# Linear attention and two feed-forward networks on one core: k-v products and the turning of k with both heads of a pair in one matmul

## Chip, core and metric

The kernel runs on one core of a Trainium2 chip. The metric is the device time of one execution in microseconds. Three runs of the kernel before gave 814.27 to 815.28 us, with a median of 814.49.

## What is computed

The reference, cut to what matters (q, k, v are float32, shaped 4 x 8 x 576 x 64):

```python
q_s = np.exp(q - np.max(q, axis=-1, keepdims=True))
q_s = q_s / (np.sum(q_s, axis=-1, keepdims=True) + 1e-09)
k_s = np.exp(k - np.max(k, axis=2, keepdims=True))
k_s = k_s / (np.sum(k_s, axis=2, keepdims=True) + 1e-09)
kv = np.einsum('bhsd,bhse->bhde', k_s, v)
x = np.einsum('bhsd,bhde->bhse', q_s, kv)       # then 2304 x 512
h = x @ w_in                                    # 512 x 2048
x2 = (h * (1.0 / (1.0 + np.exp(-1.702 * h)))) @ w_out
h = x2 @ w_in2
sp = np.where(h > 20.0, h, np.log1p(np.exp(np.minimum(h, 20.0))))
out = (h * np.tanh(sp)) @ w_out2
```

So k is normalised over the 576 positions of a head, a 64 x 64 product of k and v is made per head, and q times that product is the input of the first network.

## The kernel before

The 2304 rows are cut into five blocks (`SIZES`: 512, 512, 512, 384, 384). Attention makes the input of a block, and the networks then run over blocks of rows and 16 slices of 128 hidden columns. The networks' matmuls are split: each fp32 operand is two fp32r parts, high and low, and three matmuls make one product (`SPLIT`). They are the spine of the program, on TensorE (PE). In the first network a step n computes `gemm_in` (12 matmuls of 512 columns, L1034) and `gemm_out` (12 as well, L1103). Weights arrive as raw words and are decoded by ScalarE (ACT: L451, L415) and VectorE (DVE: L462, L475, L419), and are then split into a high copy (L405, L406) and a low remainder (L398).

Attention's steps are guests on PE between the spine's. Heads are taken in pairs, and a pair of one batch is a unit u; there are 16, of 4 batches with 4 pairs each. k of a unit lies in a tile `kt` with 96 partitions: position p*6 + c goes to partition p, slot c. Its layout is head, slot, element. The steps of a unit are:

- `k_load` (one DMA a unit) and `v_load`, all on SyncE's queue.
- The first three units (`NTURN`) use `k_first`: k is turned by 12 matmuls with the identity (L693), so that the maximum can be taken along a row (L706). ACT applies the exponential with sums (L721), PE turns it back (L732) and ACT copies it to `kt` (L741).
- The other 13 use `k_later`: the maximum is made on DVE over the 6 slots (`k_max`, L666 and L676), PE turns the remaining 96 x 128 maxima (L679), DVE reduces them (L680), PE spreads the result (L753), DVE subtracts it (L755) and ACT applies the exponential (L756).
- `k_kv` multiplies by v on PE (L769): 6 slots times 2 heads, 12 fp32 matmuls. Head j writes partitions 64*j to 64*j + 63. In the units of `k_later`, v has two more columns of ones, which give the sums of k. Then the reciprocal on DVE (L786 to L790) and two scaled copies (L798) into `kv32`, which holds both heads' products on its diagonal.
- `q_turn` turns q (L919, 4 transposes) and `x_part` multiplies it by `kv32` (L949).

Units 0 to 3 belong to the first block and run before the first network's first matmul. The 12 others belong to the blocks 1 to 3 and run as guests.

The order of all steps is not written out. The program first records them (`Plan.op`: possible engines with a cost in ns, what is read, what is written). `Plan.order` then places them engine by engine from the costs, with urgencies that `Plan.best` finds in 20 passes with random noise (`SEED`, `NOISE`). Before the spine starts it fills PE's idle time with idle transposes (L1701). A guest followed by a spine step is charged `RETURN` ns. `FIRST` and `RIGHTS` tell behind which network step the combined weights are made. So a changed cost or constant anywhere moves the order of all engines.

## Time and profile before

| what | value |
|---|---|
| runs shown, median (lowest to highest) | 814.49 us (814.27 to 815.28) |
| profiled execution, its own time | 812.75 us |
| its span, from first to last instruction | 811.0 us |
| PE matmul busy | 803.3 us (99%), 5082 records |
| PE weight loads busy | 731.9 us (90%) |
| VectorE (DVE) busy | 654.0 us (81%) |
| ScalarE (ACT) busy | 455.5 us (56%) |
| GpSimd (POOL) busy | 17.9 us (2%) |
| DMA | 208.57 MB, mean 257 GB/s |
| mean granted clock of PE, as a share | 0.999 |

Times are in microseconds. A busy engine is one on which some instruction is under way. Matmuls overlap, so their mean duration is longer than the time from one start to the next, and the second is what a matmul costs in a stream. An fp32 matmul is two records, an fp32r matmul or a transpose one. The first number of a tile shape such as 96*64 is the contraction's partitions, the second the weight's columns, and the shape behind it is the moving operand. In the timeline a row is a start, a length, and a group of like instructions with their count.

### The profile page before, as it was taken

What the parts mean: (1) busy time and instruction counts of PE and PEld (TensorE: products, weight loads), DVE (VectorE), ACT (ScalarE), POOL (GpSimd) and SP (SyncE); (2) the same over time, 40 slices, a digit from 0 to 9 for tenths busy, and PEclk for the clock granted to TensorE, in tenths of its full rate; (3) what the DMA queues carried; (4) which work ended last, traced back from release to release, by engine and by line L of the source; (5) the groups of instructions that cost most, each with busy time, mean ns of one, the idle gap of its engine ahead of it and who ended that gap; (6) DMA issues with size and microseconds to landing.
All of it is one profiled execution on the core that took longest, in us unless ns stands there. A gap on an engine that the chain in (4) does not pass through costs nothing.

```text
span 811.0 us, 14340 instructions
## 1 busy us (share of the span) xinstructions
PE 803.3 (99%) x5082; PEld 731.9 (90%) x5082; DVE 654.0 (81%) x1269; ACT 455.5 (56%) x887; POOL 17.9 (2%) x23
## 2 busy tenths in 40 slices
PE   8999999999999999999999999999999999999998
PEld 7787778877788888999999999999999999999998
DVE  7999987999966888776779779978677987677964
ACT  6998954556664565745557546555344663344542
POOL 0001000001000000000000000000000021000000
PEclk9999999999999999999999999999999999999999
DMA  9788875847777889988987998999698886778762
GB/s 248 231 258 241 266 255 166 250 136 202 233 254 263 264 264 320 319 283 264 301 264 268 293 321 274 308 318 385 179 286 298 299 293 214 227 251 265 270 195 59
DMA packets 127959, 208.57 MB, mean 257 GB/s; under 512 B 38736, under 2 KB 88464, under 8 KB 127888
## 3 DMA queue, kind: packets, MB, share of 16 engines
q1 hardware_dynamic: 127888, 207.66, 79.3%
q8 instruction: 40, 0.66, 0.3%
q14 instruction: 31, 0.25, 0.1%
HBM read 152.57 MB, written 55.05 MB: 256 GB/s over the span
## 4 chain that ended last, share of the span: by engine, by line
PE 84%; DVE 3%; DMA 1%; issue 0%; ACT 0%; DVEq 0%
PE acc L1557 22%; PE at L1327 18%; PE acc L1103 11%; PE h L1034 11%; PE h L1327 10%; PE acc L1666 5%; PE h L1666 3%; PE at L949 1%; PE at L769 1%; DMA raw<-in_moe_w_out_dram 1%; PE at L919 1%; DMA combos<-raw 1%; PE h L1557 0%; DVE kt L755 0%; DVE g L398 0%
## 5 line engine op out<-in xcount | busy, mean ns | idle before, releaser
L1034 PE MATMUL h<-xt,wi 128*128 128x512 f32 x576 | 145.0, 396 | 0.0
L1103 PE MATMUL acc<-g,wo 128*128 128x512 f32 x576 | 144.3, 394 | 0.0
L1557 PE MATMUL acc<-wi,second 128*128 128x256 f32 x1116 | 137.5, 283 | 0.0
L1557 PEld LDWEIGHTS acc<-wi,second 128*128 128x128 f32 x1116 | 135.6, 192 | 0.0
L1034 PEld LDWEIGHTS h<-xt,wi 128*128 128x128 f32 x576 | 106.5, 188 | 23.1 <-issue 1.0
L1103 PEld LDWEIGHTS acc<-g,wo 128*128 128x128 f32 x576 | 106.8, 188 | 22.7 <-issue 1.0
L1327 PE MATMUL at<-xt,wi 128*128 128x384 f32 x612 | 119.0, 335 | 0.1
L1327 PEld LDWEIGHTS at<-xt,wi 128*128 128x128 f32 x612 | 106.8, 188 | 2.8 <-DVE gt L1379 0.4
L1349 ACT ACTIVATE quad<-quad 128x384 f32<-128x384 f32 x96 | 50.2, 525 | 86.4 <-DVE quad L1379 85.8
L406 ACT ACTIVATE second<-quad 128x384 fp32r<-128x384 f32 x126 | 65.1, 523 | 47.2 <-PE acc L1557 41.8
L398 DVE TENSOR_TENSOR second<-quad,second 128x384 fp32r<-128x384 f32 x125 | 71.6, 577 | 16.3 <-ACT second L406 16.2
L1327 PE MATMUL h<-xt,wi 128*128 128x384 f32 x348 | 65.9, 334 | 0.0
L398 DVE TENSOR_TENSOR quad<-quad 128x384 f32<-128x384 f32 x96 | 53.0, 556 | 13.5 <-ACT quad L1349 11.8
L1327 PEld LDWEIGHTS h<-xt,wi 128*128 128x128 f32 x348 | 60.8, 188 | 0.0
L406 ACT ACTIVATE raw<-dec 128x512 fp32r<-128x512 f32 (+1 forms) x64 | 37.1, 600 | 20.5 <-DVE dec L398 14.8
L1327 PE MATMUL at<-wi,wi 128*128 128x384 f32 x246 | 48.3, 335 | 0.0
L1557 PE MATMUL acc<-wi,g 128*128 128x256 f32 x372 | 48.2, 283 | 0.0
L451 ACT ACTIVATE dec<-raw 128x512 f32<-128x512 f32 x62 | 41.1, 666 | 10.8 <-DMA raw<-in_moe_w_in_dram 5.5
L475 DVE CUSTOM_DVE_ANT_0 dec<-raw,dec 128x1024 uint16<-128x1024 uint16 x64 | 44.9, 703 | 1.7 <-ACT raw L415 0.2
L1557 PEld LDWEIGHTS acc<-wi,g 128*128 128x128 f32 x372 | 46.2, 192 | 0.0
L1327 PEld LDWEIGHTS at<-wi,wi 128*128 128x128 f32 x246 | 43.2, 188 | 1.0 <-DVE gt L1379 0.3
L1057 ACT ACTIVATE gt<-h 128x512 f32<-128x512 f32 x41 | 24.2, 591 | 31.9 <-PE h L1034 31.0
(191 smaller groups left out, 1158.1 us busy)
## 6 DMA issues: line engine op xcount, KB each, us to landing
wi<-combos SPq DMA_DIRECT2D x96, 512.0 KB, 4.9
wi<-outs SPq DMA_DIRECT2D x76, 512.0 KB, 5.6
raw<-in_moe_w_in_dram SPq DMA_DIRECT2D x32, 512.0 KB, 5.3
raw<-in_moe_w_out_dram SPq DMA_DIRECT2D x32, 512.0 KB, 5.4
combos<-raw SPq DMA_DIRECT2D x32, 512.0 KB, 4.1
outs<-raw SPq DMA_DIRECT2D x32, 256.0 KB, 3.8
wi<-combos SPq DMA_DIRECT2D x32, 256.0 KB, 5.2
combos<-raw SPq DMA_DIRECT2D x24, 256.0 KB, 3.8
```

What stands on the lines that cost most here:

```text
L398: return lambda: engine.tensor_tensor(out=out(), in0=in0(), in1=in1(), op=op)
L406: (ACT, act_ns(n), lambda: nc.scalar.activation(out=out(), in_=in_(), func=AF.Copy), False),
L451: lambda: nc.scalar.activation(out=f32(a), in_=f32(hi_w), func=AF.Prelu, scale=2.0**-112, alpha=2.0**32),
L475: dve(512, [rl], [da], lambda: nc.vector.tensor_tensor(out=a, in0=a, in1=lo_w, op=ALU.add), pair=True)
L769: nc.tensor.matmul(out=ps3[j * D : (j + 1) * D, 0:width], lhsT=of[:, j, c, :], rhs=w[:, j, c, :], start=c == 0, stop=c == KC - 1,)
L1034: nc.tensor.matmul(out=h(), lhsT=w_mm(fc, 0, a, cc), rhs=x_of(t)[:, cc, b, :], start=cc == 0 and i == 0, stop=cc == NCC - 1 and i == 2,)
L1057: act(nb, [hk, ("tables",)], [tk], lambda: nc.scalar.activation(out=t, in_=h, func=AF.Tanh, scale=0.851), psum=True)
L1103: nc.tensor.matmul(out=acc[dm][:, 0:nb], lhsT=w_mm(fc, 1, a, dm), rhs=g_of(n)[:, b, :], start=fc == 0 and i == 0, stop=fc == NFC - 1 and i ...
L1327: nc.tensor.matmul(out=bank_of(key)[:, 0:NB], lhsT=wt(fc, 0)[:, w : w + P], rhs=operand(k, b)[:, cc, :], start=cc == 0 and i == 0, stop=cc ...
L1349: nc.scalar.activation(out=t(), in_=t(), func=AF.Mish if n >= NPR else AF.Gelu_apprx_sigmoid)
L1557: nc.tensor.matmul(out=bank_of(banks[c])[:, at_ : at_ + 256], lhsT=slot(pr, a)[:, c * P : c * P + P], rhs=rhs(b), start=pr == 0 and i == 0 ...
L1666: nc.tensor.matmul(out=o, lhsT=w_mm(2 * n + j, 1, a, dm), rhs=g_tile(n, j)[:, b, lo:hi], start=n == 0 and j == 0 and i == 0 and (c < 4 or ...
```

## The change

Both heads of a pair stand side by side in `kt` (slot, head, element), so that one slot of both is a 96 x 128 weight. The turning of k takes that weight in one transpose per slot, 6 in place of 12 matmuls. The k-v product takes it against v of both heads side by side (128 columns, or 130 with the ones between the heads), 6 matmuls in place of 12; the two blocks off the diagonal are not read. k is loaded by one DMA per head. The planner's cost of a turning falls from 180 to 84 ns a slot, `q_turn` and `x_part` are exempt from the charge for a return (`light`), and constants of the planner, `FIRST` and `RIGHTS` differ.

```diff
-    NOISE = 400
+    NOISE = 700
...
-    RETURN = 100
+    RETURN = 90
...
                 if guests and i in self.spine:
-                    cost += self.RETURN
-                guests = guest(i)
+                    cost += 0.0 if last in self.light else self.RETURN
+                guests, last = guest(i), i
...
-    kt = [ap.tile([KP, 2, KC, D], F32, name=f"kt{i}") for i in range(2)]
+    kt = [ap.tile([KP, KC, 2, D], F32, name=f"kt{i}") for i in range(2)]
...
-    vt = ap.tile([KP, 2, KC, D + 2], F32, name="vt")
+    vt = ap.tile([KP, KC, 2 * D + 2], F32, name="vt")
...
+    vs = {u: sp.tile([KP, KC, 2 * D + 2], F32, name=f"vs{u}") for u in range(max(NTURN, 1), NHP - 1)}
...
     def k_load(u, begun):
         b, hp = divmod(u, NHP)
-        dma(
-            S * 512,
-            begun,
-            [("kt", k_tile(u))],
-            lambda: kt[k_tile(u)],
-            lambda: k[b, 2 * hp : 2 * hp + 2].rearrange("h (p c) d -> p h c d", c=KC),
-            slow=1.35,
-        )
+        for j in range(2):
+            dma(
+                S * 256,
+                begun,
+                [k_keys(u)[j]],
+                lambda j=j: kt[k_tile(u)][:, :, j, :],
+                lambda j=j: k[b, 2 * hp + j].rearrange("(p c) d -> p c d", c=KC),
+                slow=1.45,
+            )
...
             def turn(i=i, lo=lo, hi=hi):
                 for c in range(lo, hi):
-                    for j in range(2):
-                        nc.tensor.matmul(
-                            out=ps[i][j * D : (j + 1) * D, (c - lo) * KP : (c - lo + 1) * KP],
-                            lhsT=t[:, j, c, :],
-                            rhs=ident[0:KP, 0:KP],
-                            start=True,
-                            stop=True,
-                        )
-
-            pe(180 * (hi - lo), [kk], [keys[i]], turn, whole=True)
+                    nc.tensor.transpose(
+                        ps[i][:, (c - lo) * KP : (c - lo + 1) * KP],
+                        t[:, c].rearrange("p j d -> p (j d)"),
+                        ident[0:KP, 0:KP],
+                    )
+
+            pe(84 * (hi - lo), k_keys(u), [keys[i]], turn)
...
         def mm():
-            of = t.rearrange("p j c d -> p (j c d)").rearrange("p (c j d) -> p j c d", j=2, c=KC) if first else t
-            w = vd[u] if first else vt
             for c in range(KC):
-                for j in range(2):
-                    nc.tensor.matmul(
-                        out=ps3[j * D : (j + 1) * D, 0:width],
-                        lhsT=of[:, j, c, :],
-                        rhs=w[:, j, c, :],
-                        start=c == 0,
-                        stop=c == KC - 1,
-                    )
+                nc.tensor.matmul(
+                    out=ps3[:, 0:width],
+                    lhsT=t[:, c].rearrange("p j d -> p (j d)"),
+                    rhs=vd[u][:, :, c, :] if first else vs.get(u, vt)[:, c, :],
+                    start=c == 0,
+                    stop=c == KC - 1,
+                )
...
-    RIGHTS = {0: (2,), 1: (3,), 2: (4,), 4: (5,), 5: (6,), 8: (7,)}
+    RIGHTS = {0: (2,), 1: (3,), 2: (4,), 3: (5,), 5: (6,), 8: (7,)}
...
-    FIRST = (13, 16, 17, 18, 21, 22, 23, 24)
+    FIRST = (14, 17, 18, 19, 22, 23, 24, 25)
```

Line numbers of the changed kernel are some units higher: the turning is L703, the k-v product L776, the turning of q L926, the x part L956, `gemm_in` L1041 and `gemm_out` L1110.

How the order moves is shown at three places. The first is PE in the third block's attention, around a k-v product that is a guest of the first network. `acc`, `h` and `at` are PSUM banks, `xt` the block's input, `g` the activated hidden columns, `wi` and `wo` weights, and the last number the count of matmuls. Before:

```order
L1034 MATMUL h_107<-xt,wi_77 128x512 x3
L769 MATMUL at_111<-vt,kt_116 64x66 x12
L919 MATMUL at_112<-ident,qt 128x128 x4
L1034 MATMUL h_107<-xt,wi_77 128x512 x9
L949 MATMUL at_112<-qT_1_125,kv_3_123 128x4x32
```

With the change:

```order
L1041 MATMUL h_106<-xt,wi_78 128x512 x6
L926 MATMUL at_112<-ident,qt 128x128 x4
L776 MATMUL at_111<-vt,kt_116 128x130 x6
L1041 MATMUL h_106<-xt,wi_78 128x512 x6
L1110 MATMUL acc_99<-g,wo_83 128x512 x3
L956 MATMUL at_112<-qT_1_125,kv_3_123 128x4x32
```

Six matmuls of 128 output partitions take the place of 12 of 64. The product stands one network step later, and the turning of q has come ahead of it.

The second place is PE at the end of the first stage, up to the network's first matmuls (`h_106`). `kt_136` is k of pair 2, `kt_137` k of pair 3. Before:

```order
L753 MATMUL acc_101<-ident,mcol 96x128
L732 MATMUL acc_100<-ident,stage 96x128 x3
L919 MATMUL at_111<-ident,qt 128x128 x4
L1701 MATMUL h_107<-ident 128x128 x4
L769 MATMUL acc_99<-vd_139,kt_136 64x64 x12
L769 MATMUL acc_102<-vt,kt_137 64x66 x12
L919 MATMUL at_112<-ident,qt 128x128 x4
L1701 MATMUL h_107<-ident 128x128
L1034 MATMUL h_106<-xt,wi_68 128x512 x6
```

With the change:

```order
L761 MATMUL acc_101<-ident,mcol 96x128
L740 MATMUL acc_100<-ident,stage 96x128 x3
L926 MATMUL at_111<-ident,qt 128x128 x4
L926 MATMUL at_112<-ident,qt 128x128 x4
L1708 MATMUL h_107<-ident 128x128 x4
L776 MATMUL acc_99<-vd_139,kt_136 128x128 x6
L776 MATMUL acc_102<-vt,kt_137 128x130 x6
L1041 MATMUL h_106<-xt,wi_68 128x512 x6
```

Both turnings of q now stand ahead of the two products, and the network's first matmuls stand right behind them. Ahead of this piece the stage has 67 idle transposes in all, against 46 before.

The third place is ACT in the same stage, up to the first turned q of the second half. `dec` and `raw` are weights under decoding, `wi_68` is the first weight. Before:

```order
L904 ACTIVATE xt<-at_112 128x512
L415 ACTIVATE raw_88<-raw_88 128x512
L741 ACTIVATE kt_136<-acc_99 96x384
L741 ACTIVATE kt_136<-acc_100 96x384
L756 ACTIVATE kt_137<-kt_137 96x768
L406 ACTIVATE wi_68<-dec_92 128x512
L451 ACTIVATE dec_93<-raw_89 128x512
L929 ACTIVATE qT_0_124<-at_111 128x512
```

With the change:

```order
L911 ACTIVATE xt<-at_112 128x512
L729 ACTIVATE stage,ks<-acc_99,mcol 128x384
L729 ACTIVATE stage,ks<-acc_100,mcol 128x192
L456 ACTIVATE dec_93<-raw_89 128x512
L420 ACTIVATE raw_89<-raw_89 128x512
L749 ACTIVATE kt_136<-acc_99 96x384
L411 ACTIVATE wi_68<-dec_92 128x512
L749 ACTIVATE kt_136<-acc_100 96x384
L765 ACTIVATE kt_137<-kt_137 96x768
L936 ACTIVATE qT_0_124<-at_111 128x512
```

Two decoding steps of the second weight (`raw_89`) and the copy of the first have come ahead of the second copy of pair 2's k; the exponentials of pair 2 (L721 before, L729 now) stand behind both copies of x instead of between them.

## Rows read from the trace of the kernel before

**Rows 1.** The page: busy us, share of the span, instructions.
```profile
PE 803.3 (99%) x5082; PEld 731.9 (90%) x5082; DVE 654.0 (81%) x1269; ACT 455.5 (56%) x887; POOL 17.9 (2%) x23
```

**Rows 2.** Windows: stretch, length, busy us by engine, granted clock, DMA share, GB/s.
```profile
5.00:23.50 18.50, 17.05 (x237) 13.36 (x236) 18.36 (x40) 14.20 (x34) 0.00 (x0) 1.00 1.06 265
23.50:72.00 48.50, 48.50 (x212) 39.09 (x211) 47.40 (x88) 43.77 (x78) 3.41 (x2) 1.00 0.86 256
72.00:233.00 161.00, 159.90 (x971) 127.32 (x970) 144.14 (x304) 100.35 (x213) 4.34 (x4) 1.00 0.71 221
```

**Rows 3.** Waits of PE: who waited for whom, us in total, times, longest.
```profile
PE at L769 <- ACT kt L756: 0.5, 2, 0.3
PE acc L769 <- DMA vd<-in_v_dram: 0.3, 1, 0.3
```

**Rows 4.** Timeline of PE at the end of the first stage: start, length, group.
```profile
21.49 0.92 PE L769 MATMUL acc<-vd,kt 96*64 96x64 f32 x24 [0.35 <-DMA vd<-in_v_dram]
22.21 0.90 PE L769 MATMUL acc<-vt,kt 96*64 96x66 f32 x24
23.04 0.66 PE L919 MATMUL at<-ident,qt 128*128 128x128 f32 x4
...
23.57 1.63 PE L1034 MATMUL h<-xt,wi 128*128 128x512 f32 x6
```

**Rows 5.** Chain that ended last, one undisturbed step: start, length, what.
```profile
266.27 2.72 PE h L1034 x12
```

**Rows 6.** Timeline of PE around one k-v product of block 2.
```profile
161.66 2.20 PE L1034 MATMUL h<-xt,wi 128*128 128x512 f32 x9
163.79 0.92 PE L769 MATMUL at<-vt,kt 96*64 96x66 f32 x24
164.64 0.97 PE L1034 MATMUL h<-xt,wi 128*128 128x512 f32 x3
165.45 2.91 PE L1103 MATMUL acc<-g,wo 128*128 128x512 f32 x12
```

**Rows 7.** Groups of PE by shape: busy us, mean ns of one, idle before.
```profile
L769 PE MATMUL at<-vt,kt 96*64 96x66 f32 x288 | 11.1, 226 | 0.5 <-ACT kt L756 0.5
L919 PE MATMUL at<-ident,qt 128*128 128x128 f32 x48 | 7.5, 279 | 0.2
L949 PE MATMUL at<-qT,kv 128*128 128x192 f32 x16 | 4.0, 333 | 0.0
...
L919 PE MATMUL at<-ident,qt 96*128 96x96 f32 x32 | 3.7, 249 | 0.0
```

**Rows 8.** Timeline of PE: four transposes of 128 and of 96 columns, an x part of 192.
```profile
147.57 0.60 PE L919 MATMUL at<-ident,qt 128*128 128x128 f32 x4
...
196.24 0.49 PE L919 MATMUL at<-ident,qt 96*128 96x96 f32 x4
...
198.08 0.49 PE L949 MATMUL at<-qT,kv 128*128 128x192 f32 x2
```

**Rows 9.** Timeline of ACT at the end of the first stage.
```profile
19.75 0.70 ACT L415 ACTIVATE raw<-raw 128x512 int32<-128x512 uint32 x1
20.31 0.87 ACT L741 ACTIVATE kt<-acc 96x384 f32<-96x384 f32 x2
...
21.78 0.65 ACT L406 ACTIVATE wi<-dec 128x512 fp32r<-128x512 f32 x1
22.30 0.71 ACT L451 ACTIVATE dec<-raw 128x512 f32<-128x512 f32 x1
22.88 0.61 ACT L929 ACTIVATE qT<-at 128x512 f32<-128x512 f32 x1
```

**Rows 10.** Windows of two stretches of the first stage, columns as above.
```profile
8.00:10.00 2.00, 2.00 (x29) 1.62 (x24) 1.99 (x6) 1.72 (x5) 0.00 (x0) 1.00 1.10 271
14.00:16.00 2.00, 2.00 (x37) 1.60 (x37) 2.00 (x3) 1.65 (x7) 0.00 (x0) 1.00 1.33 251
```

**Rows 11.** Timeline of DVE: the first weight's second half.
```profile
22.46 0.69 DVE L398 TENSOR_TENSOR wi<-dec,wi 128x512 fp32r<-128x512 f32 x1
```

More of the change, by code (lines that the diff above doesn't have):

```diff
@@ L44, in __init__ @@
         self.spine = set()
+        self.light = set()
         self.last_write = {}
@@ L95, in order @@
         held = {DVE: 0.0, POOL: 0.0}
-        guests = 0
+        guests, last = False, None
         def guest(i):
@@ L365, in tile_attention_moe_moe @@
     make_identity(nc, ident)
-    nc.gpsimd.memset(vt[:, :, :, D : D + 2], 1.0)
+    for t in [vt, *vs.values()]:
+        nc.gpsimd.memset(t[:, :, D : D + 2], 1.0)
     plan = Plan()
@@ L380, in dve, with pe @@
         plan.op([(DVE, dve_ns(n, fast), fn, pair or fast)], reads, writes)
-    def pe(ns, reads, writes, fn, whole=False):
+    def pe(ns, reads, writes, fn, whole=False, light=False):
         if ("spine",) in writes:
             plan.spine.add(len(plan.ops))
+        if light:
+            plan.light.add(len(plan.ops))
         plan.op([(PE, ns, fn, whole)], reads, writes)
@@ L619, in k_tile, with k_keys @@
         return u if u < NHP else u % 2
+    def k_keys(u):
+        return [("kl", k_tile(u), j) for j in range(2)]
     def k_load(u, begun):
         b, hp = divmod(u, NHP)
[L623 to L630 removed]
+        for j in range(2):
[7 more added lines that the diff above has]
+            )
     def v_keys(u):
[L633 removed]
+        return [("vs", u, j) for j in range(2)] if u in vs else [("vt", j) for j in range(2)] if u >= NTURN else [("gt", 0), ("gt", 1)] if u == 0 else [("vd", u)]
     def v_load(u, begun):
@@ L761, in k_kv @@
         t = kt[k_tile(u)]
-        width = D if first else D + 2
+        gap = 0 if first else 2
+        width = 2 * D + gap
         def mm():
-            of = t.rearrange("p j c d -> p (j c d)").rearrange("p (c j d) -> p j c d", j=2, c=KC) if first else t
-            w = vd[u] if first else vt
             for c in range(KC):
-                for j in range(2):
-                    nc.tensor.matmul(
-                        out=ps3[j * D : (j + 1) * D, 0:width],
-                        lhsT=of[:, j, c, :],
-                        rhs=w[:, j, c, :],
-                        start=c == 0,
-                        stop=c == KC - 1,
-                    )
+                nc.tensor.matmul(
[5 more added lines that the diff above has]
+                )
         r = rs[:, u % NHP : u % NHP + 1]
         rk = ("rs", u % NHP)
-        pe(720, [kk] + [kk + (j,) for j in range(2)] + v_keys(u), [key3], mm, whole=True)
+        pe(720, k_keys(u) + [kk + (j,) for j in range(2)] + v_keys(u), [key3], mm, whole=True)
         if first:
@@ L791, in k_kv @@
         for j in range(2):
-            o = slice(j * D, (j + 1) * D)
+            o, e = slice(j * D, (j + 1) * D), slice(j * (D + gap), j * (D + gap) + D)
             plan.op(
@@ L923, in turn @@
                 )
-        pe(110 * NCT, keys, [key], turn)
+        pe(110 * NCT, keys, [key], turn, light=True)
         o = qT32[hp % 2][:, 0:nb]
@@ L951, in mm @@
             )
-        pe(max(1.67 * n, 440) + 20, [("kv32", hp, j) for j in range(2)] + [("qT32", hp % 2)], [key], mm, whole=True)
+        pe(max(1.67 * n, 440) + 20, [("kv32", hp, j) for j in range(2)] + [("qT32", hp % 2)], [key], mm, whole=True, light=True)
         if blk >= NDIR:
@@ L1000, in unit @@
                     k_later(u, banks[0][:, 0:P], banks[0][:, P : 2 * P], keys[0])
-                    k_kv(u, banks[1][:, 0:P], keys[1])
+                    k_kv(u, banks[1][:, 0 : P + 2], keys[1])
             else:
-                p = [at[0][:, i * P : (i + 1) * P] for i in range(3)]
+                p = [at[0][:, i * P : (i + 1) * P + 2 * (i == 2)] for i in range(3)]
                 k_later(u, p[0], p[1], ("at", 0))
@@ L1708, in tile_attention_moe_moe @@
         [("late",)]
-        + [("kt", i) for i in range(2, NHP)]
+        + [("kl", i, j) for i in range(2, NHP) for j in range(2)]
         + [("vd", i) for i in range(1, NTURN)]
+        + [("vs", u, j) for u in vs for j in range(2)]
         + [("qr", i) for i in range(2)],
@@ L1766, in tile_attention_moe_moe @@
                 [("second",)]
-                + [("kt", i) for i in range(2)]
+                + [("kl", i, j) for i in range(2) for j in range(2)]
                 + [("vt", j) for j in range(2)]
```

36 lines of the change are left out of this document (19 added, 17 removed).

## The prediction

> **What bounds the kernel now.** I read the page's busy times first, then the waits of TensorE (PE), then the windows by stage, and only then single stretches of the timeline. PE is busy 803.3 of 811.0 us, and no other engine is near that [rows 1]. The windows say from where on: from 23.5 us to the end PE has hardly a gap (48.50 of 48.50 us, then 159.90 of 161.00), at a granted clock of 1.00, the upper of its two levels (2.4 GHz) [rows 2]. Between 5 and 23.5 us it is VectorE (DVE, 18.36 of 18.50 us) and the DMA engines (share 1.06, so filled) that are fullest [rows 2]. The waits of PE after the start are small: 0.5 us in two k-v products, all for the exponential of k on ScalarE (ACT), and 0.3 us for a v load in the first stage [rows 3]. So two sums decide. One is how long attention's own matmuls (the guests) hold PE between those of the first network, since each ns of it moves the end. The other is when the network's first matmul can start, now at 23.57 us [rows 4].
>
> **Part 1, the k-v products of blocks 1 to 3.** There are 12 of them inside the PE-bound stretch. Twelve matmuls of the network take 2.72 us undisturbed [rows 5]. In the stretch with one product, 12 network matmuls run from 161.66 to 165.45, 3.79 us, so the product costs 3.79 - 2.72 = 1.07 us [rows 6]. The row of the product itself tells how that is made up. Its 24 records (12 fp32 matmuls, each in two records) last 0.92 us, the last one 0.226 of it [rows 6, 7], so from the first start to the last it is 0.69 us, about 0.058 per pair of records. The two heads, written to partitions 0 to 63 and 64 to 127, therefore run side by side. The other 0.38 us is PE emptying before the product and after it.
>
> The changed product has 6 fp32 matmuls, 12 records, each with a weight of 128 columns and 130 moving columns, and both heads are in it at once with the unused cross terms. The trace of before has no such row. The nearest from below are the transposes with 128 moving columns: four last 0.60 us, one of them 0.279, so (0.60 - 0.279) / 3 = 0.107 us each [rows 7, 8]. From above it is the x part of 192 columns, two records in 0.49 us, one of them 0.333: 0.157 us from start to start [rows 7, 8]. These are 0.84 and 0.82 ns per moving column, so the cost goes by the columns. I take 0.85 ns times 130, 0.111 us, next to the transposes. Twelve of these are 1.33 us. I charge nothing for the change of tiling, since the network's matmuls use the whole array too. The cost of one product goes from 1.07 to 1.33, and 12 x 0.26 = **+3.1 us**, all of it on the path. The ends kept for the range are 0.107 (1.28 us each, +2.6 us in all) and 0.12, which allows for 0.1 us around each product (1.44, +4.4). What would lie far below, a record at the price of today's pair, is a rival.
>
> Here the Trainium skill says otherwise. Its page "TensorE: Matmul & The Clock Gate", section "Back-to-back issue gap", gives about 81 ns per matmul of N = 128 for a sustained stream of weight loads and matmuls. By that figure 12 records would be 0.97 us as an estimate, below today's 1.07, and this part a gain of 1.2 us. The trace disagrees: 0.107 us at the same width [rows 7, 8].
>
> **Part 2, the first stage.** Three units turn k by 6 transposes instead of 12 matmuls; four products of the first batch change as in part 1. At the end of the stage the product of pair 2 starts at 21.49, that of pair 3 at 22.21, a turning of q follows at 23.04 and the network at 23.57, 2.08 us after the start of the first [rows 4]. In the new order the turning of q stands ahead of the two products and the network right behind them, so this piece becomes 2 x 1.33 = 2.66 us, **+0.6**. When the product of pair 2 can start depends on ACT: the copies of its turned k (L741) run from 20.31 on and are followed by the exponential of pair 3 and the first weight's copy [rows 9]. In the new order three more steps stand ahead of the second copy: the scaling of a weight's other half (L415, 0.56 us to the next start), the step of the next decoding (L451, 0.58) and the copy of the first weight (L406, 0.52) [rows 9], 1.66 in sum. ACT has no gap there. About 0.3 us is free, because the product now waited for its v [rows 4]. That makes 1.66 - 0.3 = 1.36 at most; some of it was done elsewhere in the queue before, so I take 1.2, **+1.2 us**.
>
> The loads bound the same point from another side. Each k pair comes by two DMAs in place of one, in pieces of 256 bytes in place of 1536, on engines that are full. In the windows the 1536-byte loads move 271 GB/s at share 1.10 (246 per full share), and a stretch with 256-byte v loads 251 at 1.33 (189) [rows 10]. The four pairs are 1.18 MB: 4.8 us at the one rate, 6.2 at the other, so up to 1.4 us later; one of pair 3's v loads now stands behind pair 2's and takes back 0.5. This lies beside the 1.2 us of ACT, not on top of it. The DMA issues that come on top on SyncE, one per unit, cost PE nothing themselves. The shorter turning is worth nothing at the end: DVE is full there, and delivers the first weight's second half at 22.46 + 0.69 = 23.15 [rows 11], so the network cannot begin much before 23.3. The stage's term is 0.6 + 1.2 = **+1.8 us**, with ends of -0.2 (all hidden behind DVE) and +3.0 (ACT and loads both late).
>
> **Part 3, the rest of the order.** The count of the network's matmuls, of q turnings and of x parts is unchanged. Guests are grouped anew, and the steps that write the combined weights are due one network step later. These have only to be ready before PE: they cost nothing as long as PE waits as little as now (0.5 us in the middle, [rows 3]). If that cover is gone, each late k stops the network, since PE works in order; I allow 1 us either way. In blocks 1 to 3 the 256-byte k loads have room, with a DMA share of 0.71 [rows 2]. The tile for early v loads is made for no unit here, since its range is empty, and costs nothing. DVE's maximum over k reads the same 384 elements per partition, and copies and products after k-v have the same sizes.
>
> **Sum.** 3.1 + 1.8 = +4.9 us. The profiled execution took 812.75 us (span 811.0), which gives 817.65. The median of the runs shown, 814.49, lies 1.74 above that execution, so I forecast **819.4 us** for the median, 0.6% slower.
>
> **Rivals.**
> - *A full-width record costs what a pair of half-width records does now* (0.058 us, [rows 6, 7]). Then a product is 0.70 us without any emptying, 12 x (0.70 - 1.07) = -4.4, and the first stage loses only its 1.2: 811.3 us, faster. For it speaks that the emptying (0.38 us a product) does go. Against it: every full-width row, transposes and x parts, costs by its moving columns [rows 7, 8]. The point that decides is 1.07 / 12 = 0.089 us per record: below it the change gains. Chance 0.07.
> - *A record costs by the partitions its operands fill, not by the columns alone.* The k-v product contracts over 96 partitions. Four transposes of q with 96 partitions and 96 columns last 0.49 us, one of them 0.249, so 0.080 us each [rows 7, 8]. At that price a product is 0.96 us, 12 x (0.96 - 1.07) = -1.3, and with +1.2 from the start 814.4, no change. Against it: 0.080 is also what 96 columns at 0.84 ns give. Chance 0.06. The rate that the Trainium skill's page named above gives would end at the same time.
> - *A late k in each unit*. Two products now wait 0.5 us together for the exponential [rows 3]. If the order of the new plan makes all 12 wait 0.3 us, 3.6 us come on top: 823.0 us. For it: ACT and DVE are over four fifths full in the stage before (43.77 and 47.40 of 48.50 us [rows 2]). Against it: the loads can be issued early. Chance 0.07.
>
> **How the numbers follow.** A measurement of this kernel tells about 0.2% (1.6 us) from no change. The forecast case has 0.80: its ends are 2.6 - 0.2 - 1.0 = +1.4 and 4.4 + 3.0 + 1.0 = +8.4, so 815.9 to 822.9, and only its lowest tenth touches "same". The range 815.8 to 823.1 takes in the forecast case and most of the late-k rival. Faster has 0.07 (the first rival). Same has 0.09 (the second rival and the low tail). Slower has 0.84.
>
> **What would show it.** Right: the k-v rows of the profile after have 12 records per product, about 0.11 us from start to start, and 12 network matmuls around one take 2.72 + 1.33; the network's first matmul starts at about 25.4 us; PE is still full behind it. Wrong: records under 0.089 us, a first matmul before 24 us, or waits of PE over 2 us in blocks 1 to 3.

## The result and the profile after

The changed kernel took 819.68 us as the median of six runs (819.34 to 819.94), the kernel before 814.35 in the runs beside it (812.47 to 815.28, six runs): a ratio of 1.0067, with a 95% interval of 1.0054 to 1.008. The profiled execution of after took 819.91 us (span 818.1). That is 7.2 us above the profiled execution of before (812.75), while the medians differ by 5.3: before's profiled execution was among its quicker ones. In the comparisons below traces are set against traces, and medians against medians.

The page of after, busy time by engine. It answers to [rows 1]:

```profile
PE 809.9 (99%) x4857; PEld 743.3 (91%) x4857; DVE 657.6 (80%) x1268; ACT 455.2 (56%) x886; POOL 22.2 (3%) x25
```

TensorE (PE) has 225 fewer instructions and is busy 6.6 us longer. So what grew is the price of the instructions, or the idle time that lies inside PE's busy spans.

The windows of after, with borders moved by about as much as the network's start. They answer to [rows 2]:

```profile
5.00:25.80 20.80, 19.70 (x158) 17.56 (x157) 19.36 (x41) 15.68 (x38) 0.00 (x0) 1.00 1.10 260
25.80:74.00 48.20, 47.97 (x209) 38.51 (x208) 47.03 (x92) 43.96 (x77) 1.42 (x1) 1.00 0.86 243
74.00:235.00 161.00, 159.79 (x805) 131.90 (x804) 141.50 (x291) 95.77 (x203) 7.56 (x6) 1.00 0.69 207
```

The clock stays at its upper level, the DMA share behind the start is no higher than before, and PE is nearly as full as before behind 25.8 us. So it is still PE's own row of work that decides, and the start of that row.

The end of the first stage on PE, from its timeline (start, length, group). It answers to [rows 4]:

```profile
21.69 1.04 PE L926 MATMUL at<-ident,qt 128*128 128x128 f32 x8
22.57 0.60 PE L1708 MATMUL h<-ident 128*128 128x128 f32 x4
23.00 1.64 PE L776 MATMUL acc<-vd,kt 96*128 96x128 f32 x12
24.48 1.57 PE L776 MATMUL acc<-vt,kt 96*128 96x130 f32 x12
25.81 1.63 PE L1041 MATMUL h<-xt,wi 128*128 128x512 f32 x6
```

The network's first matmul comes at 25.81 in place of 23.57, **+2.24 us**. The product of pair 2 starts 1.51 later (23.00 for 21.49), and from it to the network are 2.81 us in place of 2.08. L1708 are idle transposes.

One product alone among the network's matmuls, from PE's timeline of after. It answers to [rows 6]:

```profile
99.44 0.84 PE L1041 MATMUL h<-xt,wi 128*128 128x512 f32 x3
100.13 1.50 PE L776 MATMUL at<-vt,kt 96*128 96x130 f32 x12
101.39 2.29 PE L1041 MATMUL h<-xt,wi 128*128 128x512 f32 x9
103.52 0.84 PE L1110 MATMUL acc<-g,wo 128*128 128x512 f32 x3
```

Twelve network matmuls and the product last 103.52 - 99.44 = 4.08 us. Less the 2.72 of [rows 5] that is **1.36 us** a product, where it was 1.07. The 12 records last 1.50, one of them 0.276 on average, so (1.50 - 0.276) / 11 = 0.111 from start to start. Twelve products cost 12 x 0.29 = 3.5 us more.

The waits of PE in after behind the start (who waited for whom, us in total, times, longest). They answer to [rows 3]:

```profile
PE at L926 <- DVE xt L916: 1.1, 1, 1.1
...
PE h L1334 <- ACT raw L900: 0.3, 1, 0.3
```

A wait of 1.1 us is new: at 82 us a turning of q (L926) stands behind VectorE (DVE). The timeline of all engines in after there:

```profile
79.04 1.48 POOL L403 TENSOR_TENSOR wo<-dec,wo 128x512 fp32r<-128x512 f32 x1 [11.14 <-ACT wo L411]
79.29 1.38 DVE L687 TENSOR_TENSOR pmt<-pmt 96x128 f32<-96x128 f32 x1
...
81.80 0.28 DVE L687 TENSOR_TENSOR pmt<-pmt 96x128 f32<-96x128 f32 x1
...
82.00 0.21 DVE L916 TENSOR_TENSOR xt<-at,xt 128x64 fp32r<-128x64 f32 x1
...
82.27 0.66 PE L926 MATMUL at<-ident,qt 128*128 128x128 f32 x4 [1.14 <-DVE xt L916]
```

The same DVE step on 128 elements takes 1.38 us while POOL works on its subtraction and 0.28 later on, and ends within 0.2 us of POOL's end. From there to the step that PE waits for (L916) DVE's row has no gap, so the 1.1 us that DVE loses there are what PE waits for. Whether it is the order's doing or an accident is a question for the runs.

So the profile of after leaves three questions. Why does a record cost 0.111 us? How much belongs to the products and how much to the order? And what sets the start?

### The profile page after: what moved, and what is told of

Same layout as the page of the kernel before. It is cut to its first block, busy times and chain, and to the rows that moved or that the text cites. A ratio compares the mean times of both kernels' runs of the same rounds, so it can differ in the third digit from the quotient of the medians.

```text
span 818.1 us, 13930 instructions
## 1 busy us (share of the span) xinstructions
PE 809.9 (99%) x4857; PEld 743.3 (91%) x4857; DVE 657.6 (80%) x1268; ACT 455.2 (56%) x886; POOL 22.2 (3%) x25
## 4 chain that ended last, share of the span: by engine, by line
PE 88%; DVE 2%; ACT 1%; DMA 1%; issue 0%
PE acc L1564 22%; PE at L1334 18%; PE acc L1110 13%; PE h L1041 12%; PE h L1334 10%; PE acc L1673 5%; PE h L1673 3%; PE at L776 2%; PE at L956 1%; PE at L926 1%; DMA raw<-in_moe_w_out_dram 1%; DVE dec L480 0%; PE h L1564 0%; ACT dec L456 0%; DVE dec L467 0%
## 5 line engine op out<-in xcount | busy, mean ns | idle before, releaser
L1041 PE MATMUL h<-xt,wi 128*128 128x512 f32 x576 | 146.1, 397 | 0.2 <-DVE xt L916 0.2
L1110 PE MATMUL acc<-g,wo 128*128 128x512 f32 x576 | 144.9, 395 | 0.0
L1041 PEld LDWEIGHTS h<-xt,wi 128*128 128x128 f32 x576 | 106.4, 188 | 24.1 <-issue 0.8
L1110 PEld LDWEIGHTS acc<-g,wo 128*128 128x128 f32 x576 | 106.7, 188 | 22.3 <-issue 0.8
L1334 PE MATMUL at<-xt,wi 128*128 128x384 f32 x612 | 119.0, 335 | 0.1
L1334 PEld LDWEIGHTS at<-xt,wi 128*128 128x128 f32 x612 | 106.8, 188 | 2.8 <-DVE quad L1386 0.4
L403 DVE TENSOR_TENSOR second<-quad,second 128x384 fp32r<-128x384 f32 x126 | 74.7, 601 | 19.7 <-ACT second L411 19.6
L1334 PE MATMUL h<-xt,wi 128*128 128x384 f32 x348 | 66.3, 335 | 0.4 <-ACT raw L900 0.3
L1334 PEld LDWEIGHTS h<-xt,wi 128*128 128x128 f32 x348 | 60.7, 188 | 1.0 <-ACT raw L900 1.0
L1334 PE MATMUL at<-wi,wi 128*128 128x384 f32 x246 | 48.2, 335 | 0.0
L1334 PEld LDWEIGHTS at<-wi,wi 128*128 128x128 f32 x246 | 43.3, 188 | 0.8
L411 ACT ACTIVATE g<-gt 128x512 fp32r<-128x512 f32 (+1 forms) x41 | 25.7, 626 | 29.6 <-PE acc L1110 23.1
```

Of the source, the lines that this page charges most:

```text
L403: return lambda: engine.tensor_tensor(out=out(), in0=in0(), in1=in1(), op=op)
L411: (ACT, act_ns(n), lambda: nc.scalar.activation(out=out(), in_=in_(), func=AF.Copy), False),
L1041: nc.tensor.matmul(out=h(), lhsT=w_mm(fc, 0, a, cc), rhs=x_of(t)[:, cc, b, :], start=cc == 0 and i == 0, stop=cc == NCC - 1 and i == 2,)
L1110: nc.tensor.matmul(out=acc[dm][:, 0:nb], lhsT=w_mm(fc, 1, a, dm), rhs=g_of(n)[:, b, :], start=fc == 0 and i == 0, stop=fc == NFC - 1 and i ...
L1334: nc.tensor.matmul(out=bank_of(key)[:, 0:NB], lhsT=wt(fc, 0)[:, w : w + P], rhs=operand(k, b)[:, cc, :], start=cc == 0 and i == 0, stop=cc ...
```

## The experiments

A small table first, since all of them are read the same way: the span, the start of the network's first matmul, the difference of the two (all that lies behind the start), and one lone product as computed above. Each row is one trace. The fifteen executions of before beside E1 to E4 have spans of 810.0 to 812.5 us, so a difference of a microsecond between two rows can be chance. The line numbers of these kernels differ by a few from those of after.

| kernel | span | first matmul | rest | lone product |
|---|---|---|---|---|
| before | 811.0 | 23.57 | 787.4 | 1.07 |
| after | 818.1 | 25.81 | 792.3 | 1.36 |
| E1, after with a product per head | 814.0 | 25.16 | 788.8 | 1.08 |
| E2, before's order with merged products | 817.2 | 25.39 | 791.8 | 1.36 |
| E3, E2 with a product per head | 811.0 | 23.39 | 787.6 | 1.07 |
| E4, after with long pieces of k | 817.8 | 25.27 | 792.5 | 1.35 |
| E5, after again | 818.5 | 25.87 | 792.6 | 1.35 |
| E6, half of the moved columns | 817.9 | 25.87 | 792.0 | 1.37 |
| E7, two ACT steps fewer | 816.9 | 25.33 | 791.6 | 1.35 |
| E8, the same without 17 idle transposes | 817.7 | 25.36 | 792.3 | 1.35 |
| E9, 96 weight columns, 66 moved | 813.9 | 25.16 | 788.7 | 1.08 |
| E10, 64 weight columns, 66 moved | 812.8 | 24.52 | 788.3 | 1.07 |
| E11, 64 weight columns, 130 moved | 821.4 | 25.64 | 795.8 | 1.71 |
| E12, after without 17 idle transposes | 818.2 | 25.52 | 792.7 | 1.35 |

**E1, the new order with a product per head.**

```diff
-                nc.tensor.matmul(
-                    out=ps3[:, 0:width],
-                    lhsT=t[:, c].rearrange("p j d -> p (j d)"),
-                    rhs=vd[u][:, :, c, :] if first else vs.get(u, vt)[:, c, :],
...
+                for j in range(2):
+                    at_, n = j * D, D + gap
+                    nc.tensor.matmul(
+                        out=ps3[j * D : (j + 1) * D, at_ : at_ + n],
+                        lhsT=t[:, c, j, :],
+                        rhs=vd[u][:, j, c, :] if first else vt[:, c, at_ : at_ + n],
...
```

> The changed kernel and its order, with one part undone: the k-v product again takes one head at a time (12 matmuls of 64-column weights and 64 or 66 moving columns per product, written to their own 64 partitions). Layout, loads, turning and order stay. Theory (the product's records carry the loss, at 0.11 us each): in each of the 12 guests 1.35 us fall to 1.05, which is 12 x 0.30 = 3.6 us, and the two products that stand last before the network's first matmul get 0.6 to 1.2 us shorter, so 4.2 to 4.8 us less than the changed kernel: about 815.2 us, ratio to the kernel before about 1.001. Rival (the new order carries the loss, the product is neutral): no change, about 819.7 us.

Measured: 815.8 us (814.65 to 816.88, five runs) beside 812.68 for before (15 runs), a ratio of 1.0037 (1.0025 to 1.005). PE's timeline of E1 at the place shown of after:

```profile
98.67 0.84 PE L1043 MATMUL h<-xt,wi 128*128 128x512 f32 x3
99.45 0.92 PE L778 MATMUL at<-vt,kt 96*64 96x66 f32 x24
100.30 2.33 PE L1043 MATMUL h<-xt,wi 128*128 128x512 f32 x9
102.47 0.84 PE L1112 MATMUL acc<-g,wo 128*128 128x512 f32 x3
```

102.47 - 98.67 - 2.72 = 1.08: the price of before is back. What remains, 1.4 us behind the start (788.8 for 787.4) and 1.6 at the start, belongs to the order, the loads and the turning of k.

**E2 and E3, the order of before.** Both have k per head side by side, two loads for each pair and the new turning of k, but the plan of before step for step. E2 has the merged product, E3 the product per head. The core of E2 against before (E3 keeps the two matmuls per slot and only takes their operands from the new layout):

```diff
-                for j in range(2):
-                    nc.tensor.matmul(
-                        out=ps3[j * D : (j + 1) * D, 0:width],
-                        lhsT=of[:, j, c, :],
-                        rhs=w[:, j, c, :],
...
+                nc.tensor.matmul(
+                    out=ps3[:, 0:width],
+                    lhsT=t[:, c].rearrange("p j d -> p (j d)"),
+                    rhs=vd[u][:, :, c, :] if first else vs.get(u, vt)[:, c, :],
...
```

> The changed kernel's computation (layout, loads by head, turning by transposes, k-v product of both heads in one matmul) in the order of the kernel before: planner constants, costs, FIRST and RIGHTS are the old ones, and a unit's two k loads are one step of the plan. Theory (product 3.6 us in the guests, 0.6 us at the end of the first stage, the rest is order): about 814.4 + 4.2 = 818.6 us, ratio about 1.005. If the new order costs nothing, 819.7 as the changed kernel. Rival (the new order carries the loss): 814.4 us, ratio 1.000.

> As the run in the old order, but the k-v product takes one head at a time: what is left of the change is the layout, the k loads by head in pieces of 256 bytes and the turning by 6 transposes. Theory (shorter turning is worth nothing at the end of the first stage since VectorE is full, loads come a little later): 814.4 us within 0.8, ratio 1.000. If the turning were on the path, it would be up to 1 us faster; if the 256-byte loads were on the path, up to 1.4 us slower.

Measured: E2 818.38 us (817.66 to 819.68, five runs), a ratio of 1.0073 (1.006 to 1.0085). E3 813.77 us (812.4 to 814.99, eleven runs), a ratio of 1.0012 (1.0003 to 1.0021). So loads, layout and turning together cost 1.1 us by the medians, 0.2 to 1.7 by the interval; the trace of E3, one of the shorter of its eleven executions (spans of 810.6 to 813.2), shows none of it. The merged product alone costs 818.38 - 813.77 = 4.6 us by the medians. The two traces differ by more, 6.2 us, since that of E2 is the longest of its five (815.9 to 817.2): 4.2 lie behind the start and 2.0 at the start. The network's first matmul in PE's timelines of E2 and of E3:

```profile
25.39 1.63 PE L1037 MATMUL h<-xt,wi 128*128 128x512 f32 x6
23.39 1.63 PE L1039 MATMUL h<-xt,wi 128*128 128x512 f32 x6
```

Each of the four products of the first stage takes 0.44 to 0.56 us longer to the next start, for example pair 1's (15.48 to 16.82 in E2, 14.75 to 15.60 in E3). Not all of it reaches the end: the first product of E2 starts 0.40 later already, behind v's load (12.69 for 12.29), and slack on the way takes about as much back. In the new order the same exchange moves the start by only 0.65 (25.16 to 25.81). There E1's products stand still for other things: pair 2's takes 1.12 us for 0.92, and pair 3's waits 0.16 for the exponential of its k (L765).

**E4, long pieces.** After, with each load of k written to the tile in 1536 consecutive bytes for a partition and no longer in six pieces of 256, which puts k's elements into other places (heads and positions are mixed).

```diff
-                lambda j=j: kt[k_tile(u)][:, :, j, :],
-                lambda j=j: k[b, 2 * hp + j].rearrange("(p c) d -> p c d", c=KC),
+                lambda j=j: kt[k_tile(u)].rearrange("p c j d -> p (c j d)")[:, 384 * j : 384 * j + 384],
+                lambda j=j: k[b, 2 * hp + j].rearrange("(p c) d -> p (c d)", c=KC),
```

> The changed kernel, with each k load writing 1536 contiguous bytes per partition in place of 6 pieces of 256, so that slots and heads of k are mixed up in the tile and the result is that of other keys; count and size of the loads and the order stay. Theory (the end of the first stage hangs on ScalarE's copies of k, not on the loads): no change against the changed kernel, 819.7 us within 0.3. Rival (the 256-byte pieces make the first stage late): up to 1.4 us faster, 818.3 us.

Measured: 819.1 us (818.19 to 819.54), a ratio of 1.0076 (1.0062 to 1.009), and the first matmul at 25.27, 0.54 earlier than in after. So the expectation of no change missed: in this one trace the short pieces cost about half a microsecond at the start, and nothing behind it. Starts differ by some tenths of a microsecond between executions anyway, as E12 shows below, so the 0.54 may hold some of that.

**E5, after again** on the chip of the next runs:

> The changed kernel as it is, on the chip of the runs beside it. Theory (a product costs 1.35 us in place of 1.05, the first network matmul comes 2.2 us later, one wait of 1.1 us is new): 818 to 820 us, first network matmul at 25.8 us, a lone product 1.35 us, the wait on the turning of q near 81 us again. Rival (the wait of 1.1 us is an accident of one execution): 0.5 us or less of wait there, and the median 1 us lower.

Measured: 819.88 us (819.76 to 820.27, four runs) beside 813.27, a ratio of 1.0078 (1.0057 to 1.01), first matmul at 25.87. The two engines' timelines of E5 at the place of the new wait, POOL first:

```profile
78.54 2.19 POOL L403 TENSOR_TENSOR wo<-dec,wo 128x512 fp32r<-128x512 f32 x1 [10.57 <-ACT wo L411]
...
78.95 0.28 DVE L687 TENSOR_TENSOR pmt<-pmt 96x128 f32<-96x128 f32 x1
```

Here it is POOL's step that is long (2.19 for 1.48) and DVE's that is short, and PE waits for nothing there. The Trainium skill's page "SBUF — State Buffer", section "Who interferes with whom", says that DVE and GpSimd share one pair of ports under an exclusive lock, and that a DVE instruction with two inputs in SBUF contends with a GpSimd instruction that reads SBUF. Both executions agree with it: now DVE loses 1.1 us, now POOL 0.7. But the rival's lower median did not come. E5 has a wait of 1.0 us at another turning of q (at 305.81 us), and its rest is 792.6 for 792.3. The other traces in the new order show the same two cases. In E1, E4, E8, E10 and E12 DVE's step is the long one (1.38 or 1.39 us), and PE waits 0.7 to 1.2 us at the turning of q near 82 us. In E6, E7, E9 and E11 POOL's step is the long one (2.01 to 2.18), and PE waits 0.4 us there in E6 and not at all in the other three. E2 and E3 have no such wait: the new order lays these steps side by side, and who loses changes from execution to execution. What the wait costs shows in the rest of E7, which has none, 791.6 us, against 792.3 to 792.7 in E4, E8 and E12, which have 1.2.

**E6, half of the moved columns.** This is the run that contradicted my idea of the price.

```diff
-                    out=ps3[:, 0:width],
+                    out=ps3[:, 0 : D + gap],
                     lhsT=t[:, c].rearrange("p j d -> p (j d)"),
-                    rhs=vd[u][:, :, c, :] if first else vs.get(u, vt)[:, c, :],
+                    rhs=vd[u][:, 0, c, :] if first else vs.get(u, vt)[:, c, 0 : D + gap],
...
```

> The changed kernel with products that stream only the first head's 64 or 66 columns of v through the same weights of both heads; the second head's half of k-v is computed with the first head's v (left out: the second head's v). Theory (a record of a product is priced by the columns it streams, 0.111 us for 128 or 130): records 0.056 to 0.058 us apart, a lone product 0.7 us long and 0.72 dearer than nothing, so 12 x 0.6 = 7 us less: 811 to 813 us. Rival (a fixed price for one matmul, or a switch to weights of 128 columns that costs by itself): records 0.08 us or more apart, products of 1.0 to 1.3 us, 815 to 819 us.

Measured: 819.5 us (818.93 to 819.76, four runs), no better than after. PE's timeline of E6 at the same place:

```profile
99.39 0.84 PE L1041 MATMUL h<-xt,wi 128*128 128x512 f32 x3
100.07 1.45 PE L776 MATMUL at<-vt,kt 96*128 96x66 f32 x12
101.33 2.32 PE L1041 MATMUL h<-xt,wi 128*128 128x512 f32 x9
103.48 0.84 PE L1110 MATMUL acc<-g,wo 128*128 128x512 f32 x3
```

The product moves half the columns and costs 1.37 us as before the cut. So it is not the moved columns alone. The next suspect is the other half of each record, the load of its weights. In the groups of PEld by shape (busy us, mean ns of one), E6 shows:

```profile
L776 PEld LDWEIGHTS at<-vt,kt 96*128 96x128 f32 x144 | 17.5, 192 | 0.9 <-ACT kt L765 0.4
...
L926 PEld LDWEIGHTS at<-ident,qt 96*128 96x128 f32 x32 | 3.3, 142 | 0.6
```

A load of 128 columns lasts 192 ns in the product and 142 in a turning of q, which needs one record a matmul where the product needs two. The shorter load fits that the turnings of q, my yardstick, run at 0.080 us with 96 moved columns [rows 7, 8] and the product does not; why it is shorter no run shows.

**E9, E10, E11, the widths one by one.** E9 has weights of 96 columns, E10 and E11 weights of 64; E9 and E10 move 66 columns and E11 all 130. The edit of E9; E10 has 64 in place of 96, and E11 keeps the whole width of `ps3` and v besides:

```diff
-                    out=ps3[:, 0:width],
-                    lhsT=t[:, c].rearrange("p j d -> p (j d)"),
-                    rhs=vd[u][:, :, c, :] if first else vs.get(u, vt)[:, c, :],
+                    out=ps3[0:96, 0:D + gap],
+                    lhsT=t[:, c].rearrange("p j d -> p (j d)")[:, 0:96],
+                    rhs=vd[u][:, 0, c, :] if first else vs.get(u, vt)[:, c, 0 : D + gap],
...
```

> The changed kernel with products whose weights are the first 96 of the 128 columns of k and that move only the first head's 64 or 66 columns of v (left out: the last 32 columns of k's second head, and the second head's v). Theory formed after the run with half of the moved columns (a record of an fp32 product is held up by the longer of two things: its moved columns at 0.84 ns each, or the load of the next record's weights at 0.87 ns a weight column): 96 x 0.87 = 0.083 to 0.086 us from record to record, a lone product 1.0 to 1.05 us. Rival (a fixed price of 0.11 us for any full-width record, or a wait for the sum that the record before it leaves in the same place): 0.11 us, a lone product 1.35.

> The changed kernel with products of the first head alone: weights of 64 columns, 64 or 66 moved (left out: the second head's k-v product, in which zeros stand). Theory (load of weights and moved columns both at 0.84 to 0.87 ns a column; the two heads of the kernel before run side by side): 12 records 0.055 to 0.06 us apart, and with the emptying of TensorE around 64-wide weights a lone product costs 1.0 to 1.1 us, as much as both heads do in the kernel before. Rival (a fixed price of a full-width record): it does not apply to this width, and tells the same 0.058; but if the heads of before took turns and did not run side by side, records 0.029 us apart and a lone product of 0.7 us.

> The changed kernel with weights of the first head's 64 columns alone, but all 128 or 130 columns of v moved (left out: the second head's k-v product, in which zeros stand). Theory (the longer of moved columns and weight load): the moved columns decide, 130 x 0.84 = 0.109 us from record to record, a lone product 1.35 us or up to 0.35 us more for the emptying around 64-wide weights. Rival (the weight load alone sets the price): 0.058 us, a lone product 1.05.

Measured in one run each: E9 815.69 us, E10 814.59, E11 823.17, beside 813.54 for before. PE's timeline of E9 at the same place:

```profile
98.37 0.84 PE L1041 MATMUL h<-xt,wi 128*128 128x512 f32 x3
99.06 1.16 PE L776 MATMUL at<-vt,kt 96*96 96x66 f32 x12
100.02 2.32 PE L1041 MATMUL h<-xt,wi 128*128 128x512 f32 x9
102.17 1.52 PE L1110 MATMUL acc<-g,wo 128*128 128x512 f32 x6
```

The records are (1.16 - 0.247) / 11 = 0.083 us apart (0.247 is the mean length of one; the first gap is shorter, the others 0.085), and the product costs 102.17 - 98.37 - 2.72 = 1.08. With 32 weight columns fewer than E6 and the same moved columns, the price fell by a fifth. A fixed price of a record, or a wait of 0.11 us for the sum that the record before it leaves, is excluded. PE's timeline of E10:

```profile
97.56 0.84 PE L1041 MATMUL h<-xt,wi 128*128 128x512 f32 x3
98.34 0.91 PE L776 MATMUL at<-vt,kt 96*64 96x66 f32 x12
99.18 2.33 PE L1041 MATMUL h<-xt,wi 128*128 128x512 f32 x9
101.35 0.84 PE L1110 MATMUL acc<-g,wo 128*128 128x512 f32 x3
```

One head alone, 12 records, takes 0.91 us and costs 1.07, exactly what both heads with 24 records cost in before [rows 6]. The second head was free there, since the two run side by side. PE's timeline of E11:

```profile
98.88 0.84 PE L1041 MATMUL h<-xt,wi 128*128 128x512 f32 x3
99.65 1.55 PE L776 MATMUL at<-vt,kt 96*64 96x130 f32 x12
101.13 2.35 PE L1041 MATMUL h<-xt,wi 128*128 128x512 f32 x9
103.31 0.39 PE L1110 MATMUL acc<-g,wo 128*128 128x512 f32 x1
```

With 130 moved columns the moved columns decide: most records are 0.110 us apart in the trace, and the product costs 1.71 us, the emptying around 64-wide weights included. So the price from record to record is the longer of two things, the moved columns and the load of the weights, each at 0.85 to 0.91 ns a column (0.110 for 130 moved; 0.111, 0.085 and 0.058 for 128, 96 and 64 loaded). The changed product has both at about 0.11. The Trainium skill's page "TensorE: Matmul & The Clock Gate", section "LDWEIGHTS (loading the stationary operand)", gives the load as columns / 1.2 ns: 107, 80 and 53 ns for 128, 96 and 64. The 0.111 of after and E6's 0.11 agree, and so does E9's 0.083; E10's 0.058 lies a tenth above. The turnings of q do not: 128 weight columns at 0.080.

In these runs the weight columns are also the partitions that the product writes, and no run changes the one without the other. For the load speaks its own row, which shrinks with the columns in the same measure. PEld in E9 and in E10:

```profile
L776 PEld LDWEIGHTS at<-vt,kt 96*96 96x96 f32 x144 | 13.7, 165 | 1.3 <-ACT kt L765 0.6
L776 PEld LDWEIGHTS at<-vt,kt 96*64 96x64 f32 x144 | 9.3, 137 | 3.6 <-issue 1.6 <-ACT kt L765 1.2 <-ACT qT L936 0.4
```

From 128 to 64 columns that is (192 - 137) / 64 = 0.86 ns a column. Against a price by the partitions written speak the turnings of q, which write all 128 at 0.080 us.

**E7, E8, E12, the start.** E7 leaves out two of ScalarE's (ACT's) steps of the first stage (a decoding step of the second weight and the high copy of a piece of the first; zeros stand there), E8 also PE's last 17 idle transposes before the start, E12 these transposes alone. The changes with `skip` belong to E7 and E8, the last one to E8 and E12:

```diff
+        skip = m == 0 and io == 0 and fc == 1
...
-                lambda: nc.scalar.activation(
+                lambda: skip or nc.scalar.activation(
...
-            for _ in range(idle):
+            for _ in range(idle if before + idle <= 50 else 0):
...
```

> The changed kernel with two of ScalarE's steps of the first stage left out (one decoding step of the second weight's first piece, 0.7 us, and the high copy of one piece of the first weight, 0.66 us; both tiles are set to 0 instead, so the experts' weights are wrong there); the idle transposes ahead of the first product stay. Theory (ScalarE's row of steps sets when the k of the first products is ready): the second copy of pair 2's k ends 0.9 to 1.2 us earlier, but the product cannot begin before the idle transposes end, so the first network matmul is 0.2 to 0.5 us earlier, at 25.3 to 25.6 us. Rival (the loads of k in 256-byte pieces set it): the copies of k come no earlier, the first network matmul stays at 25.8 us.

> The same two ScalarE steps left out, and TensorE's last 17 idle transposes ahead of the first product too. Theory (ScalarE's row of steps): the products run as soon as the copies of k are there, the first network matmul is 0.9 to 1.2 us earlier than in the changed kernel, at 24.6 to 24.9 us. Rival (loads): 25.8 us as in the changed kernel. Rival (q's load, whose copies stand on TensorE ahead of the products): 25.3 us or later.

> The changed kernel without TensorE's last 17 idle transposes of the first stage, nothing else altered. Theory (the copies of pair 2's turned k on ScalarE set when the first of the two products ends): the product starts up to 0.2 us earlier and waits in its middle instead, and the first network matmul stays within 0.15 us of 25.8. Rival (the idle transposes themselves are in the way): 0.4 us earlier or more, 25.4 us, as in the run that also lacked two steps of ScalarE.

Measured: the first matmul at 25.33 in E7, 25.36 in E8 and 25.52 in E12; one run each, 818.68, 819.5 and 819.93 us. The end of the stage on ACT, from the timeline of after:

```profile
21.12 0.69 ACT L456 ACTIVATE dec<-raw 128x512 f32<-128x512 f32 x1
...
22.26 0.50 ACT L749 ACTIVATE kt<-acc 96x384 f32<-96x384 f32 x1
22.63 0.66 ACT L411 ACTIVATE wi<-dec 128x512 fp32r<-128x512 f32 x1
23.15 0.51 ACT L749 ACTIVATE kt<-acc 96x384 f32<-96x384 f32 x1
```

The second copy of pair 2's k (L749) starts at 23.15 and ends at 23.66, in the middle of the product that began at 23.00: the copies do hold this product, by 0.14 us (it lasts 1.64 us, and 1.50 in E8). But E8, with this timeline of PE,

```profile
20.88 0.53 PE L746 MATMUL acc<-ident,stage 128*96 128x128 f32 x3 [1.26 <-ACT stage L735]
21.24 0.27 PE L767 MATMUL acc<-ident,mcol 128*96 128x128 f32 x1
21.35 0.49 PE L746 MATMUL acc<-ident,stage 128*96 128x128 f32 x3
21.68 1.04 PE L932 MATMUL at<-ident,qt 128*128 128x128 f32 x8
22.55 1.50 PE L782 MATMUL acc<-vd,kt 96*128 96x128 f32 x12
24.00 1.61 PE L782 MATMUL acc<-vt,kt 96*128 96x130 f32 x12
25.36 1.63 PE L1047 MATMUL h<-xt,wi 128*128 128x512 f32 x6
```

gained only 0.5 us of the 0.9 to 1.2 that I expected; counted from the turning of k's sums (20.88 to 25.36, in E5 20.95 to 25.87) it is 0.44, and in E7 with the idle transposes 0.21. From 20.88 on PE's own row has no gap: the turning of k's sums, which waits for an earlier ACT step (L735), then eight turnings of q, then the products. So ACT's two steps are worth 0.2 to 0.4 us in these single traces, and then PE's own work in the new order is next.

E12 should have stayed at 25.8 and came at 25.52. The idle transposes are not the reason: as expected, the product of pair 2 starts earlier without them (22.53) and stands still in its middle instead (it lasts 1.83 us). At the turning of k's sums E12 is at 20.60 and E5 at 20.95, and from there to the network both take 4.92 us. The shift comes from further ahead: in E12 the first product starts at 11.20 and waits for nothing, in E5 it starts at 11.92 after a wait of 0.56 us for the first load of v. How the loads land differs by some tenths of a microsecond between executions, and it passes through to the network, because ACT waits 0.72 us for the product of pair 1 in both.

## Why the prediction held, point by point

**The direction and the size held**: slower by 0.67% for 0.6% forecast, 819.68 for 819.4 us. The median came out nearer than the working. The working gives +4.9 us over the profiled execution of before; trace against trace it was 7.1 (span 818.1 for 811.0). What made up for the difference is that the profiled execution of before lay 1.7 us under the median then shown, and that of after 0.2 above its own. That part of the hit is luck: beside E5, where before had 813.27, after is 6.6 us slower.

**Part 1** (+3.1 forecast, 12 records of 0.111 and nothing around them): 12 x 0.29 = 3.5, and by after against E1 792.3 - 788.8 = 3.5 behind the start. The record came out as taken, 0.111. The 0.4 more is that a product costs 1.36 and not 1.33, and the "1.07" of before is right. But a step of the reasoning fell: "the cost goes by the columns". By that step E6 had to be 7 us faster, and it gained nothing. The weights of 128 columns load for as long as the 130 columns move. I had ranked rows of one-record transposes, whose weights load faster, next to a product of two records. The number was right by luck: both limits happen to be equal at this shape.

**The emptying** (0.38 us a product, free for the full-width product): it does go. The records of after take 12 x 0.111 = 1.33 of its 1.36. It was worth 0.35 us a product (0.38 less the 0.03 that are left), and the records took 0.64 more for it (1.33 for 0.69).

**Part 2** (+1.8 forecast, first matmul at about 25.4): +2.24, at 25.81. The two products gave 0.73 for the 0.6 forecast, and the product of pair 2 began 1.51 later for 1.2. The step that failed is "This lies beside the 1.2 us of ACT, not on top of it": the loads of k and v stand ahead of the first products, ACT waits for the product of pair 1, so late loads and ACT's longer row can add up. E4 gives 0.54 for the short pieces, E8 0.44 for two of ACT's three steps; that the two add is inferred, since no run leaves out both. And the 0.6 and the 1.2 that the forecast added are no such sum in the runs. With the loads and the turning of after, the merged products alone bring the first matmul from 23.39 to 25.39 (E3, E2), the new order alone to 25.16 (E1), both together to 25.81: 2.0 and 1.8 make 2.4. That the total came near the forecast's 1.8 is in part luck.

**Part 3** (0, within 1 us): E1 against before shows 1.4 us behind the start for the new order, E1 against E3 1.2, and with merged products, as in the kernel after, after against E2 only 0.5. For that kernel the forecast holds. The cover that the prediction named, "as long as PE waits as little as now", was gone at one place: the turning of q at 82 us in seven of the eleven traces in the new order, 0.4 to 1.2 us. What the rest of the 1.4 is, no run separates; PE's 0.3 for the raw weights of the second network (L1334) is listed for after and E1 and not for before.

**The rivals.** A record at 0.058 did not come, because that price belongs to weights of 64 columns in each half of the array (E10, and E6 against it). The price by partitions is excluded too: E6, E9 and E10 all contract over 96 partitions and cost 1.37, 1.08 and 1.07. Here the figure of 81 ns from the Trainium skill's page "TensorE: Matmul & The Clock Gate", section "Back-to-back issue gap", would have given 0.97 us a product; the run shows 1.36, and the measurement decides. A late k in each unit did not come: no wait of PE on k behind the start is listed for after.

No version tried here beats the kernel before. The nearest is E3, 0.12% slower.

## What to carry to other kernels

Price a small fp32 matmul by the longer of its moved columns and its weight columns, and look at how many records it takes: merging two half-width products that already run side by side doubles both and saves only the emptying around them. Before a merged form is costed from rows of another instruction, check that the row has the same number of records and the same length of its weight load. In a stage that waits in a chain (load, product, copy, product), terms can neither be summed nor set beside each other on sight: here merged products and new order, worth 2.0 and 1.8 us alone, came to 2.4 together. Two runs, each with one of the two undone, show it.

## What was not expected

The second head of the product was entirely free in the kernel before: 12 records and 24 records both cost 1.07 us (E10 and before). Halving the moved columns of a merged product gained nothing (1.37 for 1.36), while a quarter less weight on top of that gained 0.29 (E9). And where a DVE step and a POOL subtraction meet, one of them is held up by 0.7 to 1.1 us, not always the same one (after and E5); when it was DVE, PE felt it about 2 us later in a wait of 0.7 to 1.2 us.
